# A fused top-k attention and expert layer: second fold, scatters and stores, weights and pieces put elsewhere in a hand-ordered schedule

## The chip, the cores and the metric

The kernel runs on one core of one Trainium2 chip. The metric is the device time of one launch in microseconds; a run's time is given beside the span that the profiler records on the core, from its first to its last instruction. The engines are named as in the profile: PE multiplies matrices (PEld loads its weights), DVE does vector work, ACT activations and copies out of PSUM, POOL is GpSimd, and SP issues most DMAs.

## The reference

Attention over 8 batches, 8 heads, 576 positions and a head size of 64, in which each query keeps only its 32 best keys, then a layer of 8 experts in which each of the 4608 rows of 512 goes to one expert:

```python
scores = scale * np.matmul(q, k.transpose(0, 1, 3, 2))
kth = np.partition(scores, -top_k, axis=-1)[..., -top_k:-top_k + 1]   # top_k = 32
scores = np.where(scores >= kth, scores, -1000000000.0)
attn = softmax(scores); x = attn @ v            # rows of all heads side by side: 4608 x 512
expert_idx = np.argmax(x @ w_gate, axis=1)      # 8 experts, gate_w is the softmax's largest
y = relu(x @ w1[expert]) @ w2[expert]           # 512 -> 1024 -> 512, for each row's expert
return gate_w[:, None] * y
```

All data is float32.

## The kernel before, in words

**Attention slots.** The work of attention is a list of 144 items, called slots here: 18 in each of 8 batches, 9 for each pair of head pairs (`NT = 9`, `NC = 4`). A slot is two tiles of 128 queries by 576 scores. `loop()` goes over them with index `i`; scores are multiplied three slots ahead (`AHEAD`). PE, ACT and DVE run in the order in which the Python code emits their instructions (a manual schedule); POOL's compute is kept in program order too; SP's and POOL's DMAs follow the order of emission and a priority. A buffer ring makes the next writer wait for the last reader.

**Finding the 32nd score.** `search` does this on DVE. First the scores of the next slot are folded in half: `fold` takes the larger of two halves as `h` (L320) and the smaller as `l` (L321). The *second fold*, `fold_on`, folds `h` again: the larger of its halves becomes `few` (L327) and the smaller `hl`, either on DVE (L335) or, where `aside_too` is set, on POOL with two instructions of integers (L332: sum, L333: sum less the larger). Lists of eight from `l` and `hl` (L356) are put behind `few`. Four rounds then take the best eight with MAX8 (L379) and blank them out with MATCH_REPLACE8 (L390, behind a MATCH_VALUE_LOAD), for both tiles of the slot. The callback `then` runs the second fold of the next slot. Where the flag `soon` is set it runs in round 1, otherwise before round 3.

**Which slot is which.** `loose` holds for slots 1 to 65 (`QUIET = 66`). A slot is `heavy` if POOL is to scale a finished head pair's rows in it, beside the search: L519 to L524 for the gate's logits and `rows` (L533, 128x640). `k.crowded` is set when POOL has been given a scatter, a store or rows. `soon = loose and (k.heavy or not k.crowded)`, and POOL makes `hl` where `soon` holds and the slot isn't heavy.

**Behind the search.** ACT sets `low` (L401) from the 32nd score, writes the depths (L417, twice); POOL subtracts them from the scores (L426, twice, 128x576) and notes doubtful cases (L407); ACT takes exponentials (L434), PE transposes (L445, L461), and so to the output products (L482, L493). POOL's `nbias` (L385) is issued after the first round of each search.

**Scatters and stores.** When a batch's rows are done, five indirect DMAs of POOL (L601, `scatter`) write them to `x_rows` in DRAM, sorted by expert; one is given out per slot. A finished block of the expert layer is stored by another indirect DMA of POOL (L888), which `put_stores` emits at the next slot.

**Blocks and pieces.** The expert layer works on blocks of 128 rows of one expert. Each needs its rows `xg` (L827, `load_rows`, 257 KB), `w1` (L819, 2 MB) and `w2` (L821, 2 MB, both in `load_weights`), all issued by SP; the weights have two buffers each, the rows four. `ahead()` loads a block when the block two before it begins. PE's part is 16 pieces: the first product in eight pieces (L979, 64 matmuls in the records), the second in eight (L996, 16 in the records). Between the two products of a block, `following()` has PE transpose the *next* block's rows (L868) if they count as landed. `pieces(n)` gives out `n` pieces in a slot; the rate is set anew in slot `FIRST` of a batch's 18, from the number of blocks at hand (`level`), and in the last batch from slot `ARRIVED` on.

**The end.** When attention is through, the last batch is scattered, and the blocks that are left run one behind the other with PE alone: those kept, two sure ones (one with its rows loaded early, one given as a tuple), four lengthened blocks that take up to 64 more rows (given as lists), and four plain ones, whose `piece` is a plain register value.

Of the kernel before, what the change touches and what calls it, by code (L numbers as in the profile page):

```python
# [44 lines left out]
def kernel(  # L45
# [54 lines left out]
    NC = 4  # L100
# [7 lines left out]
    NT = 2 * NC + 1  # L108
# [25 lines left out]
    k = SimpleNamespace()  # L134
# [217 lines left out]
    def lists(f):  # L352

        for m in range(2):
            for j, away in enumerate((f.l[:, m, :], f.hl[:, m, 0:QF // 2], f.hl[:, m, QF // 2:QF])):
                nc.vector.max(out=f.few[:, m, QF + 8 * j:QF + 8 * j + 8], in_=away)  # L356

    def search(tiles, s, f, then=lambda: None, soon=False, behind=lambda: None, beside=lambda: None):

        m_all = range(2)  # L360
        tops = k.small.tile([P, 2, TOP_K], F32, name="tops", bufs=4)
        if k.exact:
            src = [s[:, m, :, :].rearrange("p j k -> p (j k)") for m in m_all]
            width = S
        else:
            src = [f.few[:, m, 0:QF] for m in m_all]
            width = LW
            if not f.aside:
                lists(f)
        behind()  # L370
        scr = k.att.tile([P, 2, width], F32, name="scr", bufs=1)
        nbias = k.small.tile([P, 2], F32, name="nbias", bufs=3)
        R = TOP_K // 8

        for r in range(R):
            if r == R - 1 and not soon:
                then()
            for m in m_all:
                nc.vector.max(out=tops[:, m, r * 8:(r + 1) * 8], in_=src[m])  # L379
                if r > 1:  # L380
                    tick()
            if r == 1 and soon:
                then()
            if r == 0:
                in_turn(nc.gpsimd.tensor_scalar_mul(nbias, tops[:, :, 0], -scale))  # L385
                beside()
            if r < R - 1:
                for m in m_all:
                    first = r == 0 and not k.exact
                    nc.vector.match_replace(  # L390
                        out=src[m] if first else scr[:, m, :], in_to_replace=tops[:, m, r * 8:(r + 1) * 8],
                        in_values=src[m], imm_value=NEG,
                    )
                    if r > 1:
                        tick()
                    src[m] = f.few[:, m, :] if first else scr[:, m, :]
                if first and f.aside:
                    lists(f)
        thr = tops[:, :, TOP_K - 1]
        low = k.small.tile([P, 2], F32, name="low", bufs=3)  # L400
        nc.scalar.activation(low, thr, AF.Copy, scale=STEEP)  # L401

        def doubts():
            n, i = tiles[0]
            at = n.b * U + n.u
            over = doubt[:, at:at + 2, 2 * NC, :] if tails(tiles) else doubt[:, at, 2 * i:2 * i + 2, :]
            k.last_pool = in_turn(nc.gpsimd.tensor_tensor(  # L407
                over, f.few[:, :, QF + 7:LW:8], _inner(thr, NL), op=ALU.subtract
            )).ins

        return low, nbias, doubts
# [412 lines left out]
    def load_rows(n, piece, full=False):  # L824
        r = nc.sync.value_load(piece, min_val=0, max_val=EMPTY)
        n.x = k.mlp.tile([P, 1, XW], F32, name="xg", bufs=4)
        got = nc.sync.dma_start(n.x, xv[:, bass.ds(r, 1), :]).ins  # L827
        if not k.exact:
            for put in scattered:
                tc.add_manual_dep(got, put.name, WAIT)  # L830
            if full:
                for put in fills:
                    tc.declare_no_dep(got, put, reason="empty rows go behind all full blocks")
            fetched.append(got)
        return n
# [177 lines left out]
            evacuate()  # L1013

    PIECES = 2 * FT
    FIRST = 13
    ARRIVED = 13
    AHEAD = 3
    QUIET = 66
# [4 lines left out]
    with fast:  # L1024
# [8 lines left out]
        per_batch = len(work) // B  # L1033
        x_of, lg_of = {}, {}
        waiting, loaded, coming, spare, scatters, stores = [], [], [], [], [], []
        current = None
        left = clock = 0

        def level(b):

# [10 lines left out]
        def ahead():  # L1051
            while waiting and len(loaded) < 2:
                expert, piece = waiting.pop(0)
                if isinstance(piece, SimpleNamespace):
                    rows_in = piece
                elif isinstance(piece, list):
                    rows_in = load_half(load_rows(SimpleNamespace(), piece[0]), *piece[1:])
                elif isinstance(piece, tuple):
                    rows_in = load_rows(SimpleNamespace(), *piece, full=True)
                else:  # L1060
                    rows_in = load_rows(SimpleNamespace(), piece)
                loaded.append(load_weights(rows_in, expert))
                loaded[-1].at = clock

        def put_stores():
            while stores:
                k.crowded = True
                stores.pop(0)()

# [163 lines left out]
        def loop():  # L1233
# [9 lines left out]
            for odd in range(2):  # L1243
                for h in range(2):
                    r = slice(h * D, (h + 1) * D)
# [4 lines left out]
            for i, (b, g) in enumerate(work):  # L1250
                tiles = tiles_of(i)
                u, tile = g[0]
                if tile == 0 and u % 2 == 0:
                    open_unit(tiles[0][0])
                if tails(tiles):
                    open_unit(tiles[1][0])

                loose = 0 < i < QUIET
                k.heavy = loose and "rows" in [place for _, place in late]
                soon = loose and (k.heavy or not k.crowded)  # L1260
                then = behind = beside = lambda: None
                if i + 1 < len(work):
                    def behind():
                        f_of[i + 1] = fold(s_of[i + 1])

                    then = lambda: fold_on(f_of[i + 1], soon and not k.heavy)
                    if i:
                        behind()
                        behind = lambda: None
                if k.heavy:  # L1270
                    beside = lambda: at_place("rows")
                held = k.heavy and k.crowded
                low, nbias, doubts = search(tiles, s_of[i], f_of.pop(i), then, soon, behind, beside)
                k.crowded, k.heavy = held, False
                at_place("small")
                w_of[i] = depths(s_of[i], low)
                less(s_of.pop(i), w_of[i])
                doubts()
                at_place("pool")
                if not loose:  # L1280
                    at_place("relu")
                    at_place("rows")
                put_stores()
                scatter(1)
                at = i % per_batch
                if at == FIRST and b:
                    rate = level(b) * PIECES / (U * NT)
                credit += rate * len(g)
                room = left
                if b == B - 1 and at >= ARRIVED:  # L1290
                    room -= KEEP
                    credit = room / (len(work) - i)
                share = {0: 0.5, 1: 1.2, 2: 1.6, 3: 0.5, 2 * NC: 1.4}[tile]
                now = max(0, min(int(credit * share + 0.5), room))
                credit -= now
                clock = i
                if i + AHEAD < len(work):
                    s_of[i + AHEAD], steps = scores(got_of.pop(i + AHEAD))
                    for step in steps:
                        step()  # L1300
                if loose:
                    at_place("relu")
                evacuate()
                at_place("turn")
                turns = turning(i - 1) if i else iter(())
                next(turns, None)
                part = min(BETWEEN, now - now // 2)
                rest = pieces(part)
                next(turns, None)
                rest = pieces(now - now // 2 - part + rest)  # L1310
                weights(tiles, w_of[i], nbias)
                next(turns, None)
                evacuate()
                if i + AHEAD + 1 < len(work):
                    multiply(i + AHEAD + 1)
                if tile == NC - 1:
                    end = ending(b, u)
                    late.append([end, next(end)])
                at_place("products")
                at_place("weights")  # L1320
                credit = min(credit + pieces(now // 2 + rest), 6 * rate)
# [152 lines left out]
```

## Time and profile before

| what | value |
|---|---|
| median of 3 runs | 1285.07 us (1283.54 to 1285.09) |
| the profiled execution's own time | 1284.61 us |
| its span | 1283.0 us, 24461 instructions |
| mean granted TensorE clock | 0.967 |
| busy: PE, DVE, ACT, POOL | 1176.1, 1058.8, 933.3, 732.0 us |
| DMA moved | 220.81 MB, mean 172 GB/s |

Busy time is the sum of an engine's recorded instructions, stalls inside an instruction included. Shares of the whole span hide that the kernel has two stages: attention with pieces of the expert layer between its instructions, up to about 1047 us, and the end, in which DVE has nothing to do. Matmuls are pipelined, and their ends are modelled. A few records are missing in the trace.

### The profile page before, as it was taken

The numbers are of one execution on the slowest core, as the hardware profiler recorded it, in microseconds if no ns is written. First come the engines' busy times: TensorE is split into PE (matmuls) and PEld (weight loads), VectorE is DVE, ScalarE is ACT, GpSimd is POOL, SyncE is SP. The second block draws the span as 40 slices with busy tenths as digits, with TensorE's granted clock in tenths as the row PEclk, the third lists the DMA queues.
The fourth block names the chain that finished last, engine by engine and source line by source line (L and its number), as shares of the span: only waits on it lengthen the run. The fifth ranks groups of instructions, "written<-read, shape, count | busy, mean of one in ns | idle before, by whom it ended". The sixth has DMA issues, their size and how long they took to land. (4 is left out here: it accounts for less than half of the span.)

```text
span 1283.0 us, 24461 instructions
## 1 busy us (share of the span) xinstructions
PE 1176.1 (92%) x7574; PEld 823.6 (64%) x7574; DVE 1058.8 (83%) x4608; ACT 933.3 (73%) x2136; POOL 732.0 (57%) x884
## 2 busy tenths in 40 slices
PE   6767767898899999999999999999999999999998
PEld 3444444665566566667666666666666667789975
DVE  8999999999999999999999999999999965000000
ACT  4888887988799888888788888888888872112121
POOL 4777777786678665658555855676557743101010
PEclk9888788999899999999999999999999999999999
DMA  5001113741474147533946464547555548996582
GB/s 153 31 30 31 31 39 126 263 157 39 146 251 162 39 150 283 182 135 98 332 142 218 163 224 153 189 146 264 178 178 202 172 149 285 353 358 235 215 301 83
DMA packets 98701, 220.81 MB, mean 172 GB/s; under 512 B 5309, under 2 KB 26301, under 8 KB 98560
## 3 DMA queue, kind: packets, MB, share of 16 engines
q1 hardware_dynamic: 91360, 198.87, 44.5%
q0 software_dynamic: 6384, 19.97, 4.2%
q8 instruction: 61, 1.00, 0.3%
q14 instruction: 80, 0.66, 0.2%
q10 hardware_dynamic: 816, 0.31, 0.1%
HBM read 195.75 MB, written 24.04 MB: 171 GB/s over the span
## 5 line engine op out<-in xcount | busy, mean ns | idle before, releaser
L426 POOL TENSOR_TENSOR w<-s,w 128x576 f32<-128x576 f32 x288 | 409.2, 1441 | 317.5 <-ACT w L417 317.4
L979 PE MATMUL ph<-xTs,w 128*128 128x128 f32 x2112 | 263.0, 278 | 2.6 <-ACT xTs L870 2.6
L979 PEld LDWEIGHTS ph<-xTs,w 128*128 128x128 f32 x2112 | 251.3, 194 | 21.1 <-issue 17.6
L996 PE MATMUL py<-w,hT 128*128 128x512 f32 x528 | 248.7, 600 | 1.9 <-ACT hT L984 1.6
L434 ACT ACTIVATE w<-w,nbias 128x576 f32<-128x576 f32 x288 | 223.0, 785 | 2.3 <-POOL w L426 1.4
L445 PE MATMUL wTm<-turn,w 128*128 128x128 f32 x1152 | 173.9, 291 | 52.7 <-ACT oT L484 29.1
L417 ACT ACTIVATE w<-s,low 128x576 f32<-128x576 f32 x288 | 207.7, 768 | 4.7
L304 PE MATMUL sc<-qkb 64*128 64x288 f32 (+1 forms) x1280 | 200.7, 465 | 7.8 <-DMA qkb<-in_qk_dram 4.0
L445 PEld LDWEIGHTS wTm<-turn,w 128*128 128x128 f32 x1152 | 135.1, 148 | 111.6 <-ACT oT L484 35.5
L311 ACT COPY s<-sc 128x576 f32<-128x576 f32 x288 | 168.0, 634 | 11.9 <-PE sc L304 11.8
L379 DVE MAX8 tops<-scr 128x8 f32<-128x168 f32 x576 | 169.5, 328 | 0.0
L452 ACT COPY wT<-wTm 128x512 f32<-128x512 f32 x256 | 140.7, 596 | 37.8 <-PE wTm L445 37.2
L379 DVE MAX8 tops<-few 128x8 f32<-128x144 f32 (+1 forms) x576 | 154.9, 314 | 0.0
L304 PEld LDWEIGHTS sc<-qkb 64*128 64x128 f32 (+1 forms) x1280 | 107.1, 190 | 71.5 <-issue 35.2
L996 PEld LDWEIGHTS py<-w,hT 128*128 128x128 f32 x528 | 92.0, 191 | 86.5 <-issue 83.0
L482 PE MATMUL po<-wT,vb 128*64 128x288 f32 x1024 | 143.8, 425 | 0.0
L888 POOL DMA_INDIRECT out_dram<-y,xg x37 | 38.9, 1052 | 161.3 <-ACT y L1005 82.0
L356 DVE MAX8 few<-l 128x8 f32<-128x288 f32 x288 | 129.8, 451 | 0.0
L320 DVE TENSOR_TENSOR h<-s 128x576 f32<-128x576 f32 (+1 forms) x145 | 111.7, 770 | 3.9 <-ACT s L311 3.6
L321 DVE TENSOR_TENSOR l<-s 128x576 f32<-128x576 f32 (+1 forms) x145 | 114.3, 788 | 0.0
L482 PEld LDWEIGHTS po<-wT,vb 128*64 128x64 f32 x1024 | 70.1, 141 | 68.9 <-issue 17.4
L356 DVE MAX8 few<-hl 128x8 f32<-128x72 f32 x576 | 102.3, 221 | 0.0
(205 smaller groups left out, 1596.7 us busy)
## 6 DMA issues: line engine op xcount, KB each, us to landing
w<-in_moe_w_dram SPq DMA_DIRECT2D x74, 2048.0 KB, 9.2
qkb<-in_qk_dram SPq DMA_DIRECT2D x31, 608.0 KB, 3.8
vb<-in_v_dram SPq DMA_DIRECT2D x32, 320.0 KB, 3.2
xg<-x_rows SPq DMA_DIRECT2D x37, 257.0 KB, 9.1
x_rows<-blank SPq DMA_DIRECT2D x13, 257.0 KB, 7.9
x_rows<-blank POOLq DMA_DIRECT2D x4, 257.0 KB, 9.8
x_rows<-x,posi POOLq DMA_INDIRECT x40, 3.2
out_dram<-y,xg POOLq DMA_INDIRECT x37, 3.9
```

Source lines behind the costliest of these rows:

```text
L304: nc.tensor.matmul(ps[rows, j, 0:HF], n.q[d, cols], n.k[d, keys], start=True, stop=True)
L311: lambda m=m, ps=ps: nc.scalar.copy(s[:, m, :, :], ps[:, :, 0:HF]) for m, ps in enumerate(got)
L356: nc.vector.max(out=f.few[:, m, QF + 8 * j:QF + 8 * j + 8], in_=away)
L379: nc.vector.max(out=tops[:, m, r * 8:(r + 1) * 8], in_=src[m])
L417: nc.scalar.activation(w[:, m, :], s[:, m, :, :].rearrange("p j k -> p (j k)"), AF.Relu, scale=-STEEP, bias=low[:, m:m + 1],)
L426: k.last_pool = in_turn(nc.gpsimd.tensor_tensor(w[:, m, :], s[:, m, :, :].rearrange("p j k -> p (j k)"), w[:, m, :], op=ALU.subtract)).ins
L434: nc.scalar.activation(w[:, m, :], w[:, m, :], AF.Exp, scale=scale, bias=nbias[:, m:m + 1], accum_out=n.z[:, c:c + 1])
L445: nc.tensor.transpose(pm[:, c * P:(c + 1) * P], w[:, m, first:first + P], ident)
L452: nc.scalar.copy(wT[:, :, m, q], pm4)
L482: nc.tensor.matmul(po[r, 0:HF], n.v[:, c, r], rhs, start=(c == 0), stop=(c == KC - 1))
L979: nc.tensor.matmul(ph[:, f, :], n.w1[:, 0, dt, fc * P:(fc + 1) * P], n.xT[:, dt, :], start=(dt == 0), stop=(dt == DT - 1),)
L996: nc.tensor.matmul(py, hT[:, f, :], n.w2[:, 0, f, :], start=(f == 0), stop=(f == FT - 1))
```

## The change

Four edits, and no instruction is added or taken away: the number of instructions of each kind on each engine is the same.

1. In `search`, where `soon` holds and the slot isn't heavy, `then()` (the second fold of the next slot) comes after the MATCH_REPLACE8 pair of round 1 instead of before it. In heavy slots it stays.
2. `k.spared` is set in slots whose remainder by 9 is 2 or 7, up to slot 64. In those no stores are put and no scatter is given out; in a loose slot with remainder 6 of a batch's 18 two scatters are given out instead of one.
3. In `ahead()`, a block given as a plain value has its weights loaded first and its rows after them. The other kinds of blocks keep their order.
4. `FIRST` is 12 instead of 13.

```diff
@@ search
-            if r == 1 and soon:
+            if r == 1 and soon and k.heavy:
                 then()
...
                 if first and f.aside:
                     lists(f)
+                if r == 1 and soon and not k.heavy:
+                    then()
@@
-    FIRST = 13
+    FIRST = 12
@@
+        k.spared = False
@@ ahead
                 else:
-                    rows_in = load_rows(SimpleNamespace(), piece)
+                    loaded.append(load_rows(load_weights(SimpleNamespace(), expert), piece))
+                    loaded[-1].at = clock
+                    continue
                 loaded.append(load_weights(rows_in, expert))
@@ put_stores
-            while stores:
+            while stores and not k.spared:
@@ loop
+                at = i % per_batch
+                k.spared = 0 < i + 1 < QUIET and i % NT in (2, NC + 3)
                 put_stores()
-                scatter(1)
-                at = i % per_batch
+                scatter(1 if not loose else 0 if k.spared else 2 if at == 6 else 1)
```

## Prediction

> **What bounds the kernel now.** I first read the page's slices (part 2: the span in 40 slices of 32 us, busy tenths) for the stages.
>
> ```profile
> PE   6767767898899999999999999999999999999998
> ...
> DVE  8999999999999999999999999999999965000000
> ```
>
> Attention fills the slices in which DVE is at 9; after that PE alone works. The table of 40 us windows (window; length, then busy us of PE, PEld, DVE, ACT, POOL with their counts; clock, DMA share, GB/s) makes it exact.
>
> ```profile
> 80.00:120.00 40.00, 28.56 (x169) 17.37 (x171) 40.00 (x178) 35.04 (x84) 30.96 (x39) 0.83 0.12 40
> ...
> 1160.00:1200.00 40.00, 40.00 (x270) 39.44 (x269) 0.00 (x0) 7.28 (x13) 3.74 (x4) 1.00 0.61 221
> ```
>
> DVE has no gap from 40 us on to the end of its searches (1047 us); the list of waits of DVE names its largest in that stage as the next.
>
> ```profile
> DVE h L320 <- ACT s L311: 3.6, 4, 1.6
> ```
>
> So in attention a microsecond more on DVE is a microsecond more of span; in the last 220 us it is PE. But "busy" holds stalls: L327 takes 0.43 us at the least and 1.54 at most (the view of line L327). What stretches it is in the timeline, DVE and POOL of one ordinary slot (start, length, instruction):
>
> ```profile
> 28.50 0.46 DVE L327 TENSOR_TENSOR few<-h 128x288 f32<-128x288 f32 x1
> 28.86 0.10 DVE L390 MATCH_VALUE_LOAD scr<-tops,few 128x8 f32 x1
> ...
> 29.46 0.58 DVE L379 MAX8 tops<-scr 128x8 f32<-128x168 f32 x2
> ```
> ```profile
> 25.69 2.83 POOL L426 TENSOR_TENSOR w<-s,w 128x576 f32<-128x576 f32 x2 [1.42 <-ACT w L417]
> 28.48 0.54 POOL L407 TENSOR_TENSOR doubt<-few,tops 128x6 f32<-128x6 f32 x1
> 28.99 0.21 POOL L385 TENSOR_SCALAR nbias<-tops 128x2 f32<-128x2 f32 x1
> 29.16 0.79 POOL L332 TENSOR_TENSOR hl<-h 128x288 int32<-128x288 int32 x1
> 30.03 0.80 POOL L333 TENSOR_TENSOR hl<-hl,few 128x288 int32<-128x288 int32 x1
> ```
>
> L327 begins just as the pair L426 ends and gets through in 0.46; L407 is what waits (0.54, against a least of 0.19). Where GpSimd is first, DVE pays. At 164 us:
>
> ```profile
> 164.56 0.52 DVE L549 SCALAR_TENSOR_TENSOR oh<-lg,e_less 128x40 f32<-128x40 f32 x1
> ```
> ```profile
> 164.22 0.80 POOL L333 TENSOR_TENSOR hl<-hl,few 128x288 int32<-128x288 int32 x1
> ```
>
> L549, usually 0.18, overlaps L333 by 0.46 and takes 0.34 more: the stall is the overlap less some 0.12. L327 at 431.58 (0.82) against an L426 that ends at 432.09 gives the same.
>
> [...]
>
> **Second fold.** In 37 slots (L332 x37) GpSimd makes `hl`. There, L327 moves behind the second MATCH_REPLACE pair, 29.46 - 28.86 = 0.60 us later; the count of DVE and POOL instructions stays. L332 doesn't wait for L327, only for the last reader of the old `hl`, long past. Ordinary slot: L426 ends at 28.52; L407, no longer blocked, takes 0.21, L385 0.21, so L332 starts at about 28.88 [...]. L327, ready at 29.10, is second: overlap 0.56, stall 0.44. On DVE nothing hides it, and the search behind it, its `low` on ACT and the next slot wait too. 31 such slots: +13.6. In the other six, L426 or a store shifted the order; in five of these L327 now stalls (0.72, 0.91, 0.89, 0.82, 0.85 against 0.45: 1.95 in all) and would begin as L426 is gone: -1.95, with new collisions with L407 or L385 of about 0.1 each and one of 0.5 with a late L426 (+1.0). Sum **+12.6**; lower bound -2 (L327 still goes first), upper +15.
>
> **Scatters and stores.** `spared` slots (remainder 2 or 7 of 9) are those ahead of a slot in which GpSimd runs the rows (L533) beside the search. With a scatter in between, L533 comes late:
>
> ```profile
> 194.05 1.80 POOL L533 TENSOR_TENSOR x<-xl,rz 128x640 f32<-128x640 f32 x1
> ```
> ```profile
> 194.66 1.81 DVE L321 TENSOR_TENSOR l<-s 128x576 f32<-128x576 f32 x1
> ```
>
> L321 loses 1.06 against its usual 0.75. Without a scatter, L533 stalls the L320 ahead of it by 0.25 (1.00 against 0.74). Three batches have this (at 194.7, 322.0 and 450.7 us): -0.8 x 3 = -2.4. The scatter that moves makes two in one slot, 1.05 more on GpSimd, in whose slots it sits idle 1.4 to 1.7 us before L426; if that cover is gone, L426 and so ACT's exponent come up to 1 us late, behind three slots of lead. Two stores ahead of such a slot move too; there L321 took 0.84 and nothing stalled, so each brings 0.25 back: +0.5. Three slots lose the fold on GpSimd and three gain it: 0. Sum **-1.9**, bounds -4 and +2.
>
> **Weights ahead of rows.** SP's order was rows(n), W1(n), W2(n); it becomes W1(n), W2(n), rows(n). W2(n) waits until block n-2 has left its buffer, so the rows now sit behind that wait, about a block later; behind them on SP stand later q/k and value loads, whose own waits end later still. PE has the transposes of block n (L868) ahead of block n-1's second product (L996), so rows that are late stop PE with all that follows. At the batch starts rows waited for scatters anyway (SP stood from 869.1 to 874.0 us for one batch's); weights come there some 5 us sooner, and no wait of PE was for weights: 0. During attention the gap from the end of block n-2 to these transposes is 11 to 43 us (the new order of PE laid on the slots' times of before), against 9.7 to 11 for W2 with rows: 0, bounds 0 and +3. In the last stage it is half a block:
>
> ```profile
> 1234.01 0.37 SPq L821 DMA_DIRECT2D w<-in_moe_w_dram  x1
> 1234.61 0.39 SPq L827 DMA_DIRECT2D xg<-x_rows  x1
> 1241.15 0.37 SPq L819 DMA_DIRECT2D w<-in_moe_w_dram  x1
> 1248.46 0.37 SPq L821 DMA_DIRECT2D w<-in_moe_w_dram  x1
> ```
> ```profile
> 1240.96 0.60 PE L868 MATMUL xtp<-turn,xg 128*128 128x128 f32 x4
> 1241.40 7.03 PE L996 MATMUL py<-w,hT 128*128 128x512 f32 x16
> 1248.27 7.31 PE L979 MATMUL ph<-xTs,w 128*128 128x128 f32 x64
> 1255.41 0.60 PE L868 MATMUL xtp<-turn,xg 128*128 128x128 f32 x4
> ```
>
> By line and window, W2 issued at 1218.7, 1234.0 and 1248.5 lands 9.0, 8.8 and 9.8 us later, rows behind it 0.6 to 0.9 after: 1228.3, 1243.7, 1258.9. PE wants them at 1226.5, 1241.0, 1255.4: late by 1.8, 2.7 and 3.5. The stalls add up, as each pushes the next W2 along. The last may be 2.7, since a W1 in flight slowed that W2 and would be done. The four lengthened blocks and the two sure ones ahead of them keep rows first. One more plain block is transposed at 1084.5; its W2 (1077.5, 12.0 us on busy queues) brings rows at 1090.2: late by 5.7. Sum **+13.3**, bounds +9.5 (W2 in 9 us there, less overlap) and +14.5.
>
> **Pieces from slot 12.** PE gets the same pieces; in the order they run two to four ahead from slot 30 to about 105 and are level at the end of attention. DVE sets the pace, PE's total and its last stage stay: 0. But bursts change (8 pieces in one slot where 4 were), and the chance collisions of L327 and L320 with L426 in the second half (0.5 to 1.2 us each, some 13 in all) will fall differently: -4 to +4.
>
> **Sum.** Against the profiled execution (1284.61 with a span of 1283.0; 0.46 under the median of 1285.07): 1284.6 + 12.6 - 1.9 + 13.3 = 1308.6, or 1309 as a median. As GpSimd's timing wavers, I take a little less of the fold: **1308**.
>
> **Rivals.** (1) *The fold costs nothing*: [...] For it: 0.2 us decide. Against: the chain L407, L385, L332 has no wait in it. 1285 - 2 - 1.9 + 13.3 = 1294. (2) *Rows arrive in time*: DMA at 221 to 262 GB/s in the last windows has room, and W2 could land sooner; for a stop to vanish it must land 3 us sooner than any did. 1285 + 12.6 - 1.9 = 1296. (3) *Faster: [...].* Place: DVE's two-input instructions in attention. A later L327 clear of L426 gives the 2 above, GpSimd clear ahead of the rows 2.4, and 3 of the chance collisions go: 1278. For it: those stalls are in the trace. Against: L332 is in the way. It decides only if the rows' delay stays under 7, since that is all it can pay for. (4) *The list of who folds where merely swaps*, all else hidden: 1285.
>
> **Numbers.** The sum 0.60, rival 1 0.15, rival 2 0.13, rival 3 0.09, rival 4 0.03. A measurement tells about 0.2% (2.6 us) from no change. Slower: 0.60 + 0.15 + 0.13 = 0.88; faster 0.09; same 0.03. The first case alone reaches from 1298 to 1318 with its bounds; with rivals 1 and 2 the range is 1291 to 1318.
>
> **What would show it.** L327's mean up in the first 430 us, with L332 starting ahead of it and L407 near 0.21; L321 of 1.81 gone; PE waiting for rows at four L868 of the last 220 us, some 13 us in all. I am wrong if L327 in those slots stays at 0.46, or if no wait of PE on `xg` appears.

## The result, and the profile after

| | before | after |
|---|---|---|
| median, same chip | 1284.74 us (6 runs, 1283.54 to 1286.28) | 1319.07 us (6 runs, 1314.62 to 1324.57) |
| ratio | 1 | 1.027, 95% interval 1.0255 to 1.0286 |
| profiled execution: time, span | 1284.61, 1283.0 us | 1318.42, 1316.8 us |

The changed kernel is slower by 34.3 us. The forecast had the sign, the price of the fold and the late rows, but 1308 is 11 us too low, and 1319.07 lies just above the top of its range. In the code after the change, numbers from L399 on are two or more higher: L401 is L403, L407 is L409, L426 is L428, L868 is L870, L979 is L981, L996 is L998.

The slices of the page after (40 slices of 33 us; busy tenths of PE and DVE, and the granted TensorE clock) answer to those of before.

```profile
PE   6766767898989899999999999999999998999987
DVE  8999999999999999999999999999999933000000
PEclk9898988999999999999999999999999998999999
```

Attention is still DVE's from end to end. New are the 8s of PE in the tail and the 8 of the clock in its first full slice. What PE waited for there (engine, tile, line, releaser: total us, times, longest us), after 1070 us:

```profile
PE xtp L870 <- DMA xg<-x_rows: 10.8, 3, 6.2
PE xtp L870 <- SPq L1364: 3.3, 1, 3.3
```

Four transposes stop for rows, 14.1 us in all. In the kernel before PE stood for none; the whole list from 1062 us on is this:

```profile
PE rank L569 <- DVE pos L558: 0.5, 1, 0.5
```

The timeline of PE around the first (start, length, instruction, and in brackets the idle time before it):

```profile
1105.41 1.08 PE L870 MATMUL xtp<-turn,xg 128*128 128x128 f32 x4 [6.22 <-DMA xg<-x_rows]
1106.29 9.08 PE L998 MATMUL py<-w,hT 128*128 128x512 f32 x16
1115.21 7.31 PE L981 MATMUL ph<-xTs,w 128*128 128x128 f32 x64
```

and around the third and the fourth:

```profile
1269.36 0.63 PE L870 MATMUL xtp<-turn,xg 128*128 128x128 f32 x4 [2.89 <-DMA xg<-x_rows]
1269.82 7.03 PE L998 MATMUL py<-w,hT 128*128 128x512 f32 x16
```
```profile
1287.35 0.63 PE L870 MATMUL xtp<-turn,xg 128*128 128x128 f32 x4 [3.35 <-SPq L1364]
1287.81 8.73 PE L998 MATMUL py<-w,hT 128*128 128x512 f32 x16
```

The stops are not the whole price. Behind the stops of 6.22 and 3.35 us the second product takes 9.08 and 8.73 us, not 7.03, and the transposes behind the first 1.08, not 0.60. Behind that of 2.89 nothing is stretched. The windows of these stretches (window; length, busy us of PE, PEld, DVE, ACT, POOL; clock, DMA share, GB/s) say why:

```profile
1105.40:1115.40 10.00, 9.99 (x22) 4.83 (x23) 0.00 (x0) 0.59 (x1) 0.49 (x1) 0.75 1.04 245
1287.30:1296.50 9.20, 9.15 (x22) 4.24 (x23) 0.00 (x0) 0.59 (x1) 0.00 (x0) 0.81 0.00 0
```

The mean clock is 0.75 and 0.81 there. The two second products and the transposes lose 2.05 + 1.70 + 0.48 = 4.2 us by it.

In attention, the slot shown in the prediction now reads, DVE and POOL:

```profile
28.84 0.83 DVE L327 TENSOR_TENSOR few<-h 128x288 f32<-128x288 f32 x1
```
```profile
28.22 0.20 POOL L409 TENSOR_TENSOR doubt<-few,tops 128x6 f32<-128x6 f32 x1
28.39 0.22 POOL L385 TENSOR_SCALAR nbias<-tops 128x2 f32<-128x2 f32 x1
28.56 0.80 POOL L332 TENSOR_TENSOR hl<-h 128x288 int32<-128x288 int32 x1
29.82 0.79 POOL L333 TENSOR_TENSOR hl<-hl,few 128x288 int32<-128x288 int32 x1 [0.46 <-DVE few L327]
```

L409 gets through in 0.20, L332 starts 0.28 us ahead of L327 and runs to 29.36: overlap 0.52, stall 0.38 (0.83 against 0.45). Against the kernel before, the k-th `low` (one per search) comes 6.6 us later at slot 26, 12.4 at slot 65, 14.1 at the last, slot 143. The tail adds the rest, 19.7 us, of a span that is 33.8 longer.

### The profile page after: what moved, and what is told of

It is laid out like the page before. It is cut to its first block, busy times and chain, and to the rows that moved or that the text cites. A ratio compares the mean times of both kernels' runs of the same rounds, so it can differ in the third digit from the quotient of the medians.

```text
span 1316.8 us, 24466 instructions
## 1 busy us (share of the span) xinstructions
PE 1181.5 (90%) x7574; PEld 824.1 (63%) x7574; DVE 1072.6 (81%) x4608; ACT 936.3 (71%) x2136; POOL 717.9 (55%) x884
## 5 line engine op out<-in xcount | busy, mean ns | idle before, releaser
L428 POOL TENSOR_TENSOR w<-s,w 128x576 f32<-128x576 f32 x288 | 408.5, 1439 | 334.6 <-ACT w L419 334.5
L981 PE MATMUL ph<-xTs,w 128*128 128x128 f32 x2112 | 262.7, 278 | 2.4 <-ACT xTs L872 2.4
L981 PEld LDWEIGHTS ph<-xTs,w 128*128 128x128 f32 x2112 | 250.2, 193 | 22.2 <-issue 18.8
L998 PE MATMUL py<-w,hT 128*128 128x512 f32 x528 | 252.7, 609 | 1.1 <-ACT hT L986 0.6
L447 PE MATMUL wTm<-turn,w 128*128 128x128 f32 x1152 | 170.1, 287 | 57.6 <-ACT oT L486 30.9
L379 DVE MAX8 tops<-scr 128x8 f32<-128x168 f32 x576 | 168.9, 325 | 0.0
L379 DVE MAX8 tops<-few 128x8 f32<-128x144 f32 (+1 forms) x576 | 154.5, 312 | 0.0
L998 PEld LDWEIGHTS py<-w,hT 128*128 128x128 f32 x528 | 93.7, 194 | 87.7 <-issue 85.2
L320 DVE TENSOR_TENSOR h<-s 128x576 f32<-128x576 f32 (+1 forms) x145 | 110.3, 761 | 4.0 <-ACT s L311 3.4
L321 DVE TENSOR_TENSOR l<-s 128x576 f32<-128x576 f32 (+1 forms) x145 | 110.9, 765 | 0.0
```

The costliest lines, as they stand in the source:

```text
L428: k.last_pool = in_turn(nc.gpsimd.tensor_tensor(w[:, m, :], s[:, m, :, :].rearrange("p j k -> p (j k)"), w[:, m, :], op=ALU.subtract)).ins
L447: nc.tensor.transpose(pm[:, c * P:(c + 1) * P], w[:, m, first:first + P], ident)
L981: nc.tensor.matmul(ph[:, f, :], n.w1[:, 0, dt, fc * P:(fc + 1) * P], n.xT[:, dt, :], start=(dt == 0), stop=(dt == DT - 1),)
L998: nc.tensor.matmul(py, hT[:, f, :], n.w2[:, 0, f, :], start=(f == 0), stop=(f == FT - 1))
```

## The experiments

Every ratio stands against the kernel before on the same chip (medians 1284.4 to 1285.3). "Delay at slot k" is how much later than in the kernel before the `low` of slot k starts in the profiled execution, taken from the trace. Slots count from 0. It compares single executions: in the six kernels that leave the code up to slot 26 as it was before, the delay there lies between -1.1 and +0.7, so differences of about 1 us can be chance.

**Rows and weights: the third edit undone, and alone.** The changed kernel with rows ahead of weights again:

```diff
-                    loaded.append(load_rows(load_weights(SimpleNamespace(), expert), piece))
-                    loaded[-1].at = clock
-                    continue
+                    rows_in = load_rows(SimpleNamespace(), piece)
```

> The changed kernel with its third edit undone: rows, then W1 and W2 for every block, as before; fold, scatters and FIRST stay changed. Theory (rows behind W2 stop PE four times in the last stage, and the clock halves after the longer stops): the waits of L870 on xg, 14.1 us in the profile after, are gone, and with them the slow second products behind them (9.1 and 8.7 us instead of 7.0, 3.8 us) and the slow transposes (0.5): 1319 - 18 = 1301 us. Rival (the waits only show what the clock or attention causes elsewhere): some 1310 us or more.

Measured: 1297.81 us, ratio 1.0098 (1.0079 to 1.0116). The list of PE's waits in the tail has no wait for rows left; the delay at slot 143 stays at 13.7. So the edit costs some 21 us, nearly all of it in the tail, and more than the 18 us of stops and slow products that were expected. Alone, as the reverse of that diff on the kernel before:

> The kernel before with the weights ahead of the rows alone. Theory: four waits of the transposes for rows in the tail, 13 to 14 us, and two halvings of TensorE's clock after the longer of them, 4 to 5 us, with up to 3 us in the attention: 1302 to 1306. Rival: most of that needs the other edits' later arrival at the tail; alone the rows come in time or the waits are under 8 us: 1285 to 1293.

Measured: 1302.96 us, ratio 1.0155 (1.0137 to 1.0173), slower by 18 us in the medians and 20 by the ratio. The waits of PE from 1060 us on:

```profile
PE xtp L868 <- DMA xg<-x_rows: 10.2, 3, 5.7
PE xtp L868 <- SPq L1360: 3.6, 1, 3.6
```

13.8 us, and attention is no slower than before (delay at slot 143: -1.6). The rows are late without any help of the other edits, and the products behind the stops are slow here too:

```profile
1088.83 1.09 PE L868 MATMUL xtp<-turn,xg 128*128 128x128 f32 x4 [5.75 <-DMA xg<-x_rows]
1089.71 9.04 PE L996 MATMUL py<-w,hT 128*128 128x512 f32 x16
```

**Is it the clock?** In the changed kernel PE gets products of zeros (6, 1, 3 and 3 of them) just ahead of the four transposes, so that it doesn't stand.

```diff
+        for _ in range(fillers.get(len(fetched_plain), 0)):
+            nc.tensor.matmul(ps[...], ident, blank[:, 0:SM], start=True, stop=True)
...
```

> The changed kernel with idle matmuls of zeros (128x512) put on PE ahead of the four transposes that wait for rows in the last stage: 6 for the first stop of 6.2 us, then 1, 3 and 3; each should take 0.88 us, less than the stop it lies in, and their results are overwritten. Theory (PE's granted clock halves after the longer stops, which costs 4 us beyond them): the stops stay as long in all, but the second products behind them take 7.0 us each, and the time falls by 4 us to 1315 us. Rival (the slow products have another cause, such as DMA traffic): 9.1 and 8.7 us stay, and the time is 1319 us or a little more.

Measured: 1313.79 us, ratio 1.0236 (1.0219 to 1.0253), just below the changed kernel's interval. The first of the four places, PE's timeline (the second product is L1004 here):

```profile
1093.66 5.32 PE L870 MATMUL xtp<-blank,turn 128*128 128x512 f32 x12
1100.16 0.66 PE L875 MATMUL xtp<-turn,xg 128*128 128x128 f32 x4 [1.19 <-DMA xg<-x_rows]
1100.65 7.03 PE L1004 MATMUL py<-w,hT 128*128 128x512 f32 x16
```

The idle products and the wait left behind them make 6.5 us, so the rows come as late as ever, but the product behind them takes 7.03 again, as the one behind the fourth place does too. The clock of this stretch:

```profile
1095.00:1105.00 10.00, 8.81 (x25) 3.92 (x24) 0.00 (x0) 0.59 (x1) 2.26 (x4) 1.00 1.06 339
```

It is whole, with the DMA engines as full (share 1.06) as in the slow stretch of the changed kernel (1.04), so their traffic isn't what slowed the product. The tail is 4.8 us shorter. That is the price of the clock, shown apart from the wait. The span is 10 us shorter; the other 5 are in attention, in which the two kernels run the same code, and are taken up under "Pieces from slot 12". The median's 5.3 is the better size.

**The fold: undone, and alone.** Undone in the changed kernel:

```diff
-            if r == 1 and soon and k.heavy:
+            if r == 1 and soon:
                 then()
...
-                if r == 1 and soon and not k.heavy:
-                    then()
```

> The changed kernel with its first edit undone: the second fold back ahead of the MATCH_REPLACE pair; the rest stays changed. Theory [...]: L327 back to about 0.45 us in most of them, the searches end 12 to 13 us sooner, 1306 us. Rival (the 12.7 us of attention come from where scatters, stores and pieces went): no more than 3 us less, 1316 us.

Measured: 1310.58 us, ratio 1.0213 (1.0193 to 1.0232), between the two expectations. The delay is 0.1 at slot 26 and 0.3 at slot 65, against 6.6 and 12.4 with the fold moved, but 3.6 at slot 143. That is what the second and fourth edits leave (4.5 in the run with those two alone, below). Alone on the kernel before:

> The kernel before with the second fold's move alone. Theory: 31 slots with L327 held for 0.4 us each, less the five stalls of L426 that go: 8 to 12.5 us, 1293 to 1297. Rival: its price needs the other edits (scatters and row loads that put GpSimd beside VectorE at that time), and alone it is within 3 us of before: 1282 to 1288.

Measured: 1297.05 us, ratio 1.0099 (1.0082 to 1.0115), 12.6 us slower. The delay grows by some 0.38 at a time, to 14.4 at slot 65, and from slot 69 to 143 it stays within 11.9 to 12.4. In 34 slots L332 now starts ahead of L327 and is still running when L327 starts; in the kernel before it does so in none. L327 in the first 430 us, in the view of its line (count: least/median/longest ns), for before, after and the fold alone:

```profile
L327 DVE TENSOR_TENSOR few<-h x61: 426/451/1203, 10.0 to 425.0; 128x288 f32<-128x288 f32 x61
```
```profile
L327 DVE TENSOR_TENSOR few<-h x59: 426/831/1612, 9.3 to 423.3; 128x288 f32<-128x288 f32 x59
```
```profile
L327 DVE TENSOR_TENSOR few<-h x59: 428/815/1170, 10.0 to 423.0; 128x288 f32<-128x288 f32 x59
```

The move nearly doubles the median. Two runs test whether it is the overlap that stretches L327. In the first, POOL's first instruction reads what L327 writes, so POOL can't be first:

```diff
-            in_turn(nc.gpsimd.tensor_tensor(hl, one, other, op=ALU.add))
-            in_turn(nc.gpsimd.tensor_tensor(hl, hl, more, op=ALU.subtract))
+            in_turn(nc.gpsimd.tensor_tensor(hl, one, more, op=ALU.subtract))
+            in_turn(nc.gpsimd.tensor_tensor(hl, hl, other, op=ALU.add))
```

> The changed kernel, with the two GpSimd instructions of the second fold taken in the other order: first one half less the larger, then plus the other half. L327 stays behind the MATCH_REPLACE pair, but the first GpSimd instruction now needs its result and can't start ahead of it. Theory [...]: L327 takes about 0.45 us again in those slots, attention ends some 12 us sooner, 1307 us, though the order on every engine is that of the changed kernel. Rival (the place of L327 in DVE's order costs by itself, or GpSimd's later start stalls the next slot's L320): no gain, 1315 to 1320 us.

Measured: 1317.32 us, ratio 1.0256 (1.024 to 1.0272): nothing gained, as the rival had it. L327 is at 446 ns in the median, but the view of L320 has a new line:

```profile
  POOL hl L333: 10.6, 30
```

DVE now stands before L320, 30 times for 10.6 us, since L333 reads the one buffer of `h` to the end. The stall had only moved. The run shows that L327's stretch goes when L332 isn't ahead of it (446 ns against 831); its time can't tell what the overlap costs, as POOL's later end holds DVE instead. In the second, L332 and L333 run over half of their columns:

```diff
+            one, other, more = (t[:, :, 0:QF // 2] for t in (one, other, more))
+            half = hl[:, :, 0:QF // 2]
...
```

> The changed kernel, with GpSimd's two adds L332 and L333 over half of their columns (and the third list read from the half that is there, so the second half's smaller scores are left out). Theory: [...] L332 starts 0.27 us ahead of it and takes 0.80, so at half the length (0.4 us) it ends about 0.1 us into L327, which then takes 0.45 instead of 0.84; 31 slots by 0.4 give back about 12 us: 1307. Rival: the later place of the second fold costs something that doesn't hang on the adds' length (VectorE's own order, the lists that come late); then L327 stays above 0.7 or the time stays at 1316 to 1320.

The time, 1697.62 us (ratio 1.3213, 1.3188 to 1.3238), is no measure of the stall: the kernel leaves out part of the smaller scores, other work followed from it, and TensorE had 9506 products to do instead of 7574, all of the surplus behind attention. The slots before are comparable. There L327 starts 0.29 us behind POOL's first add (L334 in this kernel), as with the full one:

```profile
28.73 0.48 POOL L334 TENSOR_TENSOR hl<-h 128x144 int32<-128x144 int32 x1
```
```profile
29.02 0.51 DVE L327 TENSOR_TENSOR few<-h 128x288 f32<-128x288 f32 x1
```

It takes 0.51, and so it is with most; the view of its line for the first 430 us:

```profile
L327 DVE TENSOR_TENSOR few<-h x60: 429/502/1636, 9.8 to 427.2; 128x288 f32<-128x288 f32 x60
```

The delay at slot 26 is 1.4, against 6.6. Same order, same place, but a first add of 0.48 us instead of 0.80: L327 takes 0.51 instead of 0.83, so the stall goes with the length of POOL's add.

**Scatters and stores.** The scatters' half of the second edit, the stores' half, and both, each on the kernel before:

```diff
...
-                scatter(1)
+                scatter(1 if not loose else 0 if k.spared else 2 if at == 6 else 1)
```

> The kernel before with no scatter in the spared slots and two at slot 6 of a batch; the stores, the fold, the weights and the slot of the first piece stay as before. Theory: the three stalls of L321 (slots 27, 45, 63) go at 1.1 to 1.2 us each and nothing comes back: minus 3.5, 1281. Rival: the scatter that is given out later meets VectorE in another slot and the time is that of before, 1284 to 1287.

Measured: 1282.15 us (22 runs), ratio 0.9985 (0.9978 to 0.9991). The delay falls by 1.05, 1.05 and 1.06 at slots 27, 45 and 63, and the long L321 is gone. Its line in the first 470 us, before and in this run:

```profile
L321 DVE TENSOR_TENSOR l<-s x68: 452/760/1809, 7.1 to 466.2; 128x576 f32<-128x576 f32 x66, 128x288 f32<-128x288 f32 x2
```
```profile
L321 DVE TENSOR_TENSOR l<-s x68: 451/749/834, 7.1 to 464.2; 128x576 f32<-128x576 f32 x66, 128x288 f32<-128x288 f32 x2
```

The gain, 1.9 us by the ratio, is less than these three steps. One reason is on record: the stalls don't come in every execution. Seven profiled kernels have the same code as the kernel before up to slot 27, itself among them, and the stall of slot 27 is in four of their traces. In the run with pieces from slot 12 alone (below), L533 starts 0.03 us behind L320, as it did 0.04 behind in the kernel before, and this time it loses to L321 as well:

```profile
194.18 2.49 POOL L533 TENSOR_TENSOR x<-xl,rz 128x640 f32<-128x640 f32 x1
```
```profile
194.80 0.74 DVE L321 TENSOR_TENSOR l<-s 128x576 f32<-128x576 f32 x1
```

This version has the lowest median of the study, 0.15% below the kernel before.

```diff
-            while stores:
+            while stores and not k.spared:
...
```

> The kernel before with the stores left out of the spared slots alone. Theory: the stores wait for the next slot and nothing else moves: within 1 us of before, 1284 to 1285. Rival: the store's issue lands beside work of the next slot that waits for it (slots 34, 40 and 52 of the trace with both edits): plus 5 to 7, 1289 to 1292.

Measured: 1283.31 us (13 runs), ratio 0.9992 (0.9981 to 1.0003): not told from nothing.

> The kernel before with the whole second edit (scatters and stores) alone. Theory: the scatters' 2 us and the stores' 1 us are apart from each other, so they add: minus 3, 1281 to 1282. Rival: the stores' 1 us was chance, and the time is that of the scatters alone, 1282 to 1283, or they collide and it is that of before, 1284.5.

Measured: 1283.97 us (21 runs), ratio 0.9989 (0.9981 to 0.9996). This lies between the two values that the rival gives. The second edit as a whole gains 1.4 us; nothing shows that the stores add to the scatters.

**Pieces from slot 12.** First the second and fourth edits together, which is the changed kernel without the fold and the rows:

> The changed kernel with the fold and the row loads both as before, so the scatters, the stores and the pieces from slot 12 alone. Theory: these two edits carry what the other two leave of the 34 us: the stalls at slots 27, 45 and 63 go (minus 3.5) and stalls at the slots to which stores and adds have moved (32, 34, 40, 52 and after 65) come in for 5 to 8 us: 1287 to 1290. Rival: these edits are worth minus 2 to 0 as forecast, and what is left of the 34 us lies in half-clock stretches that fall by chance: 1282 to 1285.

Measured: 1289.26 us, ratio 1.0039 (1.0024 to 1.0055). The L321 stalls at slots 27, 45 and 63 are gone, and still it is 5 us slower. Which of the two edits costs it is told by the fourth alone:

```diff
-    FIRST = 13
+    FIRST = 12
```

> The kernel before with FIRST at 12 alone. Theory: the pieces of the blocks fall into other slots from slot 31 on, and with them VectorE's evacuations and GpSimd's L426 and L533; this carries the cost that the scatters and stores leave of the run with both edits (1289.3 against 1282.2 with the scatters alone): plus 6 to 7, 1290 to 1292. Rival: the stores carry it and this edit is free as forecast: 1283 to 1286.

Measured: 1294.14 us, ratio 1.0078 (1.0065 to 1.0091): 10 us for a number, and more than the 6 to 7 expected. The delay is about 0 up to slot 26 and -0.6 from 27 to 31 (the stall of slot 27 is missing), then climbs in places: +2.4 at slot 32, +0.9 at 34, +2.1 at 50. In slot 34, DVE and POOL, first in this run:

```profile
248.90 1.47 DVE L327 TENSOR_TENSOR few<-h 128x288 f32<-128x288 f32 x1
```
```profile
247.28 2.77 POOL L426 TENSOR_TENSOR w<-s,w 128x576 f32<-128x576 f32 x2 [1.63 <-ACT w L417]
```

and in the kernel before:

```profile
247.83 0.91 DVE L327 TENSOR_TENSOR few<-h 128x288 f32<-128x288 f32 x1
```
```profile
245.64 2.78 POOL L426 TENSOR_TENSOR w<-s,w 128x576 f32<-128x576 f32 x2 [2.12 <-ACT w L417]
```

There the L426 pair began 2.19 us ahead of L327, here 1.62, and L327 takes 0.56 longer: 0.56 of the 0.9. I summed by line the time from each DVE instruction's start to the next's, over slots 31 to 143, and took the difference to before: L379 +2.4 (waits for the next scores behind it), L335 +2.4, L327 +2.3, L674 +1.4, L549 +0.6, against L320 -1.7 and L321 -1.4; all that is left comes to 1.4, of +7.4. The numbers of instructions are the same. The tail adds 0.7 us.

The expectation of the run before this one named a rival: stretches of half clock. The traces have them, and the kernel's cost goes with them. Nine of the profiled kernels have `FIRST` at 12, with nearly the same attention but for the second fold, the scatters and the stores. At slot 50 the delay steps by 2.1 us in the six of them (this run among them) in which the clock record (the trace's list of the clock granted to TensorE over time) has a half-clock stretch that begins in slot 48, and by 0.5 in the three in which it has none. This run, and the run of the second and fourth edits at the same place (window; length, busy us with counts of PE, PEld, DVE, ACT, POOL; clock, DMA share, GB/s):

```profile
359.30:362.70 3.40, 3.40 (x14) 2.80 (x16) 3.40 (x12) 3.04 (x8) 3.18 (x3) 0.50 1.05 407
```
```profile
358.40:361.80 3.40, 3.40 (x29) 2.11 (x29) 3.40 (x12) 3.37 (x9) 1.98 (x4) 1.00 1.04 405
```

At half clock PE gets 14 products done in 3.4 us, at full clock 29. It is the same at slot 32 (+1.9 to +4.1 in the four with a stretch that begins in slot 30, +0.5 to +0.7 in the five without) and from slot 65 to 69 (+0.7 to +2.5 in the seven with one that begins in slot 66, -0.8 in the two without). None of the eight kernels with `FIRST` at 13 or 14 has a stretch that begins in slot 30, 48 or 66. This run has all three, and against the kernels without them they go with about 5 of its 6.8 us of delay. So with the earlier start half clock comes up in three new places, in some executions and not in others. The stalls of the list above may be how DVE comes to feel it. That the halved clock is the cause is not shown: no run changes the clock in attention.

One slot in the other direction:

> The kernel before with FIRST at 14, one slot later instead of earlier. Theory one: what counts is how GpSimd's long instructions (L426, L533) fall against VectorE's L327, L335 and L321 from slot 31 on, which any shift draws anew: a change of either sign up to 7 us. Theory two: the earlier start itself costs (more pieces in the slots of the batch's beginning, where VectorE is full), so a later start gives as much: 1278 to 1281. Rival to both: the slot is worth nothing, 1283 to 1286.

Measured: 1289.73 us, ratio 1.0052 (1.0037 to 1.0067). The profiled execution, the fastest of the six, has a delay of 2.7 at slot 143 and a tail that is 1.1 us longer. So a later start doesn't give back what an earlier one costs; 13 is better than both neighbours, in this schedule. The number acts on two things, the slot of the new rate and the rate. Each apart:

```diff
-    FIRST = 13
+    FIRST = 12
...
-            sums[-1] = (have - KEEP / PIECES) / (len(sums) - 1 + (per_batch - FIRST) / per_batch)
+            sums[-1] = (have - KEEP / PIECES) / (len(sums) - 1 + (per_batch - 13) / per_batch)
```

> The kernel before with the new rate taken at slot 12 of a batch and the rate itself worked out as before (with 13). Theory: the start one slot earlier moves the pieces, and the whole price of e9 is here: plus 7 to 10, 1292 to 1295. Rival: the rate carries it, and this run is within 3 us of before.

Measured: 1295.04 us, ratio 1.0075 (1.006 to 1.0089). The other way round, `FIRST` at 13 and 12 in the formula:

> The kernel before with the rate worked out with 12 and its start left at slot 13. Theory: the rate differs by a few per cent, some pieces fall a slot later or earlier, and the time is within 3 us of before: 1282 to 1287. Rival: the rate carries the price of e9: plus 7 to 10, 1292 to 1295.

Measured: 1288.42 us, ratio 1.0024 (1.0015 to 1.0033). The start alone has the whole price; the rate alone costs 3 us, just outside what was expected of it, and the two don't add.

## Why the prediction was right or wrong

Two terms of the sum failed: the price of PE's four stops, put at the length of the stops alone (+13.3, measured +19.9), and the pieces from slot 12, put at 0 (measured +10.0). Each edit alone, from its ratio times 1284.7 (by the medians the third is +18.3 and the fourth +9.5):

| step | forecast | alone |
|---|---|---|
| Second fold | +12.6 | +12.7 |
| Scatters and stores | -1.9 | -1.4 |
| Weights ahead of rows | +13.3 | +19.9 |
| Pieces from slot 12 | 0 | +10.0 |
| sum | 24.0 | 41.2 |
| all four together | 24 | 34.7 |

**Second fold: right**, in mechanism and size. In the slot shown L332 was to start 0.22 us ahead of L327 and to stall it by 0.44; it started 0.28 ahead and the stall was 0.38. That the sum meets 12.7 to 0.1 us is luck: alone, L327's own time grows by 10.6 us in the first 470, in 34 slots rather than 31, and a stall at slot 27 adds 1.0. That a stall is the overlap less some 0.12 us was an estimate from two stalls of the profile before, of L549 and L327; it holds in the slot shown (0.52 less 0.38 is 0.14), and with adds of half the columns, the first of them 0.48 us instead of 0.80 long, L327's median goes from 831 to 502 ns. In company it is worth less: undoing it in the changed kernel gives 8.5 us by the medians and 7.3 by the ratios.

**Scatters and stores: right in size, in part by luck.** In the profiled execution the three stalls of L321 were worth 3.2 rather than 2.4: the forecast let L533 stall L320 by 0.25 instead, and in the run with the scatters alone L533 ends ahead of L320 in all three slots, and L320 takes 0.73 or 0.74. But the forecast took the stalls of one execution for those of all, and they aren't in every one; the two errors go against each other. The stores' +0.5 is within the noise.

**Weights ahead of rows: the wait was right, the price of a wait was not.** The four stops were put at 5.7, 1.8, 2.7 and 3.5 and came at 6.2, 1.7, 2.9 and 3.3. That the rows come in only behind W2 was taken from two loads of the trace of before, in which they landed 0.6 and 0.9 us after it, and these stops bear it out to about 0.5 us. What the sum lacked, and so put at nothing, is a term for what a stop does to the work behind it, 4 to 5 us of halved clock. The sum took PE to be at full clock in the tail, as it was in the kernel before, where no wait of PE behind 1062 us is over 0.5 us (clock 1.00 from 1120 to 1280 us). In the two traces above, stops of 5.75 and 6.22 us, and of 3.35 and 3.63, were followed by halved clock, and those of 1.63 to 2.89 were not; these two traces have no stop between 2.89 and 3.35, and the ends of PE's work, from which stops are counted, are modelled. Against the run with rows first, the tail is 19.2 us longer (19.7 in span, 0.5 of it in attention); stops and clock make 18.3 of it, and for 0.9 us I have no place.

**Pieces from slot 12: wrong.** The step that failed is "0". "DVE sets the pace, PE's total and its last stage stay" is true and does not bear on the matter; the sentence behind it, that the collisions of the second half "will fall differently: -4 to +4", has a mechanism that the runs do show (L327 and L335 together are 4.7 us longer in slots 31 to 143), but bounded it too narrowly. It had no term for the clock: stretches of half clock, at places where only kernels with `FIRST` at 12 have them, go with about 5 us. The two aren't told apart, so how the cost comes about is open. Alone it was +10, +6.7 for slot 14, and +3.1 for the rate: every shift tried cost time, where the forecast was centred on none. What 13 has over its neighbours the profile of before doesn't show; it stays open too.

**The sum.** Single prices add to 41, and the four together cost 34.7. The runs say where the 6.5 us go. The second and fourth edits together cost 5.0, where their single prices make 8.6: -3.6. The fold on top of these two costs 7.6 (12.6 less 5.0), not 12.7: -5.1. The weights on top of the three cost 22.1, not 19.9: +2.2. Why the fold is cheaper with the others isn't shown; I suspect that a L327 moved back by 0.6 us gets clear of some of the late L426. Part of the difference between executions is chance, and half clock goes with it: in attention after 215 us the record has 27 us of it in the changed kernel's profile and 7 in that with PE kept busy, and most of the 5 us between the two arises in steps of 1.4 to 1.7 at slots 32, 50 and 68.

**The rivals.** None of them came. The fold wasn't free, the rows weren't in time, and the gains that rival 3 counted on were real only for the scatters.

## What to carry to other kernels

Price a stop of TensorE as the stop and the halved clock that may follow it (here the second product behind a stop of 6.22 us took 2.05 us more and that behind 3.35 took 1.70 more, while that behind 2.89 took no more); a queue on which one load waits for a buffer should carry first what is wanted first (here the rows behind W2 stopped PE for 14.1 us in all). Where an instruction of one engine takes longer while one of another runs, as L327 here (0.83 us with L332 ahead of it, 0.46 with L332 behind it), lay the start of one against the end of the other slot by slot: an order that is right by 0.3 us is lost by a move of 0.6. In a schedule tuned by hand, a shift of where background work falls is not free because totals stay; a range for it should be as wide as the stalls in the trace, with more room on the side of loss, and a stall seen in one execution should be looked for in a second before it is counted as a gain.

## What was not expected of the hardware

- The clock record of the changed kernel's profile has halved clock in stretches of 3.41 or 6.83 us alone, but for the one in which it ends (3.64): at the 6.22 us stop it stands at one half for 6.8 us, from 1.8 us before the stop ends, and behind the 3.35 us stop for 3.4. One 16-matmul product loses 1.7 to 2.05 us by it.
- Six products of zeros ahead of a late transpose kept the clock (1.00 from 1095 to 1105 us): the product behind it took 7.03 us after a stop of 1.19, against 9.08 after one of 6.22.
- As far as these two places show, the first 0.1 us or so of an overlap costs nothing: L327 took 0.51 with an overlap of 0.19 and 0.83 with one of 0.52, against 0.43 at the least.
- With the same code and the same start to within 0.01 us against L320, L533 got in ahead of L321 in one execution (1.80 for L533, 1.81 for L321) and behind it in another (2.49 and 0.74).
